# A new order of the steps on every engine, with new PSUM banks and six steps on other engines, in an attention and gated convolution kernel

## The chip, the cores and the metric

One core of a Trainium2 chip. The metric is the device time of one execution in microseconds (us), as the median of several runs; less is better. A measurement of this kernel tells a change of about 0.3% (0.7 us) from none.

## The reference: what is computed

Attention in which each query sees only the keys of its own cluster, followed by a feed-forward layer with a gated convolution along the sequence. Batch 4, 8 heads, 768 tokens, head size 64, 16 clusters; width 512, inner width 1024.

```python
q_assign = argmax(einsum('bhsd,hcd->bhsc', q_n, c_n))   # cluster of each query; k_assign likewise
mask = q_assign[:, :, :, None] == k_assign[:, :, None, :]
scores = where(mask, q @ k.T / sqrt(D), -1e9)
x = softmax(scores) @ v                                  # heads side by side: (4, 768, 512)
h = maximum(x @ w_in, 0)
conv_out = sum(conv_w[i] * h shifted by i - 1 along the sequence, i = 0, 1, 2)
out = (h * sigmoid(conv_out)) @ w_out
```

## The kernel before: tiles, stages and what sets the order

The attention works on 16 **groups** g (batch and pair of heads) and 32 **slots** t (a group and one half of its queries; a batch has 8 slots). The feed-forward layer follows batch by batch, while the attention of the next batches runs, so all engines hold both kinds of work for most of the span.

The order is written out in one long string, `PLAN`, of some 1650 tokens. `step` turns each token into the instructions of a function, and each engine executes its own in the order in which they stand there. No scheduler changes it; semaphores only make an engine wait. A token `T.3.0@2` carries indices and, behind the @, the PSUM bank (0 to 3, and 4 to 7 at the two ends), and a letter d, a or p says which engine copies: VectorE (DVE), ScalarE (ACT) or GpSimd (POOL). The tokens that the text speaks of, with the lines of the profile before:

- `_wz` (L665, L666) sets the operand of the dummy matmuls and a scratch column on DVE; `_k.n` (L663) issues n dummy matmuls on TensorE (PE), whose result nobody reads; `_zp`/`_zd` (L709) clear part of an `ext` buffer on POOL/DVE; `_id` makes the identity on POOL, `_par` (L668) reads it on DVE; `_n3` transposes the centroids.
- `LQ`, `LK`, `LV` load on SP's queue. `T.g.c` (L277) transposes four blocks of q and k of group g on PE, `Qa`/`Qd` (L233, L235) copy them to `qkT`; for the last six groups `D.g.o` (L285) transposes on DVE instead. `CDa`/`CDp`, `CQp` and `CVp` (L233, L235) cast q, k and v to half precision.
- `A.g` (L318): products of tokens and centroids on PE. `M0.g` to `M6.g` (L342 to L381): the argmax on DVE, ending in a `pack` of cluster numbers and their squares; groups 0 and 1 do it for each head apart (`M1.0.1`). `K.g` (L386) transposes the pack on PE, `Ba`/`Bd` copy it, `BX.g` sends it by DMA as three extra rows of `ext`, which make the mask part of the score product.
- `S.t.i` (L413): scores of slot t, in two double banks; `E.t.i` (L425): exponentials on ACT; `V.t.u` (L444): product with v; `NR.t` (L455) and `N.t` (L460): normalisation on DVE, which frees V's bank; `X`, `Y`, `XD`: the transposed x.
- `I` (L498) first feed-forward product, `R` (L511 on ACT, L513 on DVE) relu, `aw/bw/cw` and `a/b/c` (L530, L532) the three taps on DVE, `H` (L560) tanh on ACT, `G` (L569) gate on DVE, `O` (L581) second product, `F` and `FX` output.

For group 0 the first part reads: `T.0.0`, `T.0.1`, `T.0.2` with their copies, ten dummies, `A.0`, then the argmax of each head, while `T.1.*` runs on PE.

Of the kernel before, what the change touches and what calls it, by code (L numbers as in the profile page):

```python
# [177 lines left out]

# [686 lines left out]
```

## Time and profile before

| | us |
|---|---|
| median of 3 runs (lowest, highest) | 242.31 (241.92, 242.58) |
| the profiled execution | 240.97 |
| its span on the core | 239.2 |
| PE busy in the span | 228.5 |
| DVE busy | 209.8 |
| ACT busy | 209.5 |
| POOL busy | 71.0 |

The profile is of one execution. Its page gives the busy time of each engine; the chain of waits follows the work that ended last back from step to step; the timeline lists instructions with their start, length and the idle time ahead of them (in brackets, with what ended it); the table of stretches gives busy time between two times. Matmuls overlap, so that neighbours on PE are told by the distance of their starts.

### The profile page before, as it was taken

The numbers are of one execution on the slowest core, as the hardware profiler recorded it, in microseconds if no ns is written. First come the engines' busy times: TensorE is split into PE (matmuls) and PEld (weight loads), VectorE is DVE, ScalarE is ACT, GpSimd is POOL, SyncE is SP. The second block draws the span as 40 slices with busy tenths as digits, with TensorE's granted clock in tenths as the row PEclk, the third lists the DMA queues.
The fourth block names the chain that finished last, engine by engine and source line by source line (L and its number), as shares of the span: only waits on it lengthen the run. The fifth ranks groups of instructions, "written<-read, shape, count | busy, mean of one in ns | idle before, by whom it ended". The sixth has DMA issues, their size and how long they took to land.

```text
span 239.2 us, 6261 instructions
## 1 busy us (share of the span) xinstructions
PE 228.5 (96%) x2420; PEld 145.5 (61%) x2420; DVE 209.8 (88%) x417; ACT 209.5 (88%) x326; POOL 71.0 (30%) x120
## 2 busy tenths in 40 slices
PE   7889899999999999989999999999999999999993
PEld 6757567676766775645566556655656666665541
DVE  5689677766989999999999999999899999999950
ACT  3757899898999999989999999997999999987841
POOL 7348690974944004360200340007120000000000
PEclk9999999999999999999999999999999999999999
DMA  8966979899995957796578957885491104022233
GB/s 153 217 154 171 292 192 313 268 225 230 267 229 164 192 96 140 111 152 135 154 144 148 133 129 167 197 135 102 110 249 38 33 3 175 4 88 88 90 132 132
DMA packets 97481, 36.79 MB, mean 154 GB/s; under 512 B 88745, under 2 KB 91305, under 8 KB 97452
## 3 DMA queue, kind: packets, MB, share of 16 engines
q1 hardware_dynamic: 96524, 36.17, 66.4%
q8 instruction: 19, 0.31, 0.6%
q10 hardware_dynamic: 928, 0.23, 0.5%
q14 instruction: 10, 0.08, 0.1%
HBM read 23.11 MB, written 6.29 MB: 123 GB/s over the span
## 4 chain that ended last, share of the span: by engine, by line
PE 65%; DVE 24%; issue 4%; DMA 3%; SPq 1%; ACT 1%; DVEq 0%; ACTq 0%
PE sc L413 18%; PE flex L581 12%; PE flex L498 11%; PE flex L444 10%; DVE cnv L532 5%; PE flex L277 4%; DVE hg L569 3%; PE flex L318 3%; PE tail L581 3%; DMA qk_in<-in_k_dram 2%; PE tail L498 2%; DVE sim L342 2%; DVE val L357 2%; DVE qkT L285 2%; DVE hpad L513 1%
## 5 line engine op out<-in xcount | busy, mean ns | idle before, releaser
L425 ACT ACTIVATE attn<-sc 128x768 f16<-128x768 f32 x192 | 148.1, 829 | 8.7 <-PE sc L413 7.4
L413 PE MATMUL sc<-ext 128*128 128x384 f16 x384 | 90.4, 325 | 0.3
L532 DVE SCALAR_TENSOR_TENSOR cnv<-hpad,cwcol,cnv 128x768 f16<-128x768 f16 (+2 forms) x72 | 62.4, 890 | 0.1
L444 PEld LDWEIGHTS <-attn 128*128 128x128 f16 x1152 | 50.9, 97 | 17.3 <-issue 2.7
L444 PE MATMUL flex<-v,attn 128*128 128x65 f16 x1152 | 55.0, 193 | 0.4 <-DVE sim L342 0.4
L498 PE MATMUL flex<-xT,w_in 128*128 128x384 f16 x228 | 45.5, 325 | 0.3 <-DVE x L460 0.2
L235 POOL CAST c<-qkT 128x768 f16<-128x768 f32 x21 | 21.4, 1027 | 76.6 <-DVE qkT L285 22.9
L413 PEld LDWEIGHTS <-ext 128*128 128x128 f16 x384 | 31.3, 97 | 20.4 <-issue 7.9
L581 PE MATMUL flex<-w_out,hg 128*128 128x512 f16 x160 | 42.3, 379 | 0.0
L498 PEld LDWEIGHTS <-w_in 128*128 128x128 f16 x256 | 24.1, 97 | 16.2 <-issue 1.0
L569 DVE SCALAR_TENSOR_TENSOR hg<-th,hpad 128x768 f16<-128x768 f32 (+3 forms) x34 | 31.1, 919 | 0.4 <-ACT th L560 0.3
L581 PEld LDWEIGHTS <-hg 128*128 128x128 f16 x192 | 17.7, 98 | 16.2 <-issue 0.6
L560 ACT ACTIVATE th<-cnv 128x768 f32<-128x768 f16 (+2 forms) x30 | 25.9, 864 | 1.2 <-DVE cnv L532 1.0
L235 POOL CAST v<-v_in 128x768 f16<-128x768 f32 x16 | 15.9, 997 | 18.9 <-DMA v_in<-in_v_dram 14.1
L511 ACT ACTIVATE hpad<-flex 128x384 f16<-128x384 f32 x39 | 19.5, 536 | 0.4 <-PE flex L498 0.4
L277 PE MATMUL flex<-id,qk_in 128*128 128x128 f32 x120 | 17.5, 277 | 1.6 <-DMA qk_in<-in_k_dram 0.9
L460 DVE TENSOR_TENSOR x<-flex,rec 128x384 f16<-128x384 f32 x32 | 17.5, 547 | 0.2
L277 PEld LDWEIGHTS flex<-id,qk_in 128*128 128x128 f32 x120 | 13.4, 141 | 4.0 <-issue 1.1
L318 PE MATMUL flex<-qkT,cT 128*32 128x384 f32 x128 | 13.6, 498 | 1.6 <-DVE qkT L285 0.8
L235 DVE COPY qkT<-flex 128x512 f32<-128x512 f32 x15 | 10.1, 686 | 5.4 <-PE flex L277 5.3
L530 DVE TENSOR_SCALAR cnv<-hpad,cwcol 128x768 f16<-128x768 f16 (+2 forms) x36 | 14.5, 411 | 0.3 <-ACT th L560 0.2
L233 ACT ACTIVATE qkT<-flex 128x512 f32<-128x512 f32 x15 | 8.7, 603 | 5.3 <-PE flex L277 5.3
(81 smaller groups left out, 210.2 us busy)
## 6 DMA issues: line engine op xcount, KB each, us to landing
v_in<-in_v_dram SPq DMA_DIRECT2D x16, 384.0 KB, 4.6
ext<-c SPq DMA_DIRECT2D x24, 192.0 KB, 3.2
out_dram<-o_sb SPq DMA_DIRECT2D x9, 512.0 KB, 2.8
qk_in<-in_q_dram SPq DMA_DIRECT2D x20, 192.0 KB, 3.1
qk_in<-in_k_dram SPq DMA_DIRECT2D x9, 384.0 KB
qk_in<-in_k_dram SPq DMA_DIRECT2D x24, 96.0 KB, 2.3
qk_in<-in_q_dram SPq DMA_DIRECT2D x24, 96.0 KB, 3.8
w_sb<-in_moe_w_in_dram SPq DMA_DIRECT2D x4, 512.0 KB, 4.4
```

Of the source, the lines that this page charges most:

```text
L235: (nc.vector if name == "d" else nc.gpsimd).tensor_copy(out=to, in_=src)
L277: nc.tensor.transpose(bank[at][:, P * i : P * (i + 1)], qk_t[g][:, o, P * j : P * (j + 1)], id128[:])
L318: nc.tensor.matmul(bank[at][32 * j : 32 * (j + 1), 0:HS], lhsT=cT32[:, g % NPR, :], rhs=tokens[:, j], start=True, stop=True, skip_group_ch ...
L413: nc.tensor.matmul(s[:, n, 0:HS], lhsT=ext_b[g % NE][:, h, 1, P * (kt + n) : P * (kt + n + 1)], rhs=ext_b[g % NE][:, h, 0, HS * a : HS * ( ...
L425: nc.scalar.activation(attn[t, i // 3][:, kt : kt + 2, :], sc[(6 * t + i) % 2][:, :, 0:HS], AF.Exp, scale=0.125)
L444: nc.tensor.matmul(avp(at)[:, u, 0 : D + 1], lhsT=attn[t, h][:, kt, P * jq : P * (jq + 1)], rhs=v16_b[g % NE][:, h, kt, 0 : D + 1], start= ...
L498: nc.tensor.matmul(bank[at][:, 0:HS], lhsT=w_in16[:, r, 2 * u + f, :], rhs=xT[:, b % 2, r, HS * a : HS * (a + 1)], start=(r == 0), stop=(r ...
L511: nc.scalar.activation(to, src, AF.Relu)
L532: nc.vector.scalar_tensor_tensor(out=cnv, in0=src, scalar=w, in1=cnv, op0=ALU.mult, op1=ALU.add)
L560: nc.scalar.activation(th, cnv_t[key].rearrange("p (f s) -> p f s", s=N), AF.Tanh, scale=0.5)
L569: nc.vector.scalar_tensor_tensor(out=hg_b[b][:, 2 * u + fs.start : 2 * u + fs.stop, lo : lo + N], in0=th, scalar=1.0, in1=hpad(b, u)[:, fs ...
L581: nc.tensor.matmul(bank[at][:, 0:Dm], lhsT=hg_b[b][:, fb, P * tq : P * (tq + 1)], rhs=w_out16[:, fb, :], start=(fb == 0), stop=(fb == NFB ...
```

## The change

The string `PLAN` is replaced: 1654 tokens for 1656, in another order on each engine, 355 of them with another bank or name. Six steps go to another engine: the copies `Qa.0.0`, `Qd.0.1`, `Qd.5.0`, `Qd.6.2` become `Qd.0.0`, `Qa.0.1`, `Qa.5.0`, `Qa.6.2`; the relu `Ra.0.0` becomes `Rd.0.0`; the clearing `_zp.1.1` becomes `_zd.1.1`. `_wz` stays on DVE but goes behind `_par`. The dummy matmuls go from 113 to 87: the first burst from 35 to 14, the others by five in all.

Besides, the number 24 is taken out of the argmax's sixth step and put into the table that the fourth multiplies with, so that the sixth has one arithmetic operation for two; and `transposes`, `load` and `argmax` get branches for the groups in `RUNS` and `PSUM_PAIRS`, which are both empty, so that no group takes them.

```diff
+PSUM_PAIRS = ()
+RUNS = ()
...
-    "_wz _zp.0.1 LQ.0.0 _zd.1.0 _hpk.0 _zp.1.1 _id _zd.4.0 _par LQ.0.1 LK.0.1 _pk.2 _hz.3 _v.0 _zp.0.0 _v.2 "
-    "_hz.1 _cent lk.0.0 _n0 _n1 _nq _n2 _k.35@4 T.0.0@1 Qa.0.0 T.0.1@0 _id16 Qd.0.1 T.0.2@2 _n3@1 _n4 Qa.0.2 "
+    "_hz.1 _pk.2 _zp.0.1 LQ.0.0 _zd.1.0 _hpk.0 _zd.1.1 _id _zd.4.0 _par _wz LQ.0.1 LK.0.1 _v.0 _v.2 _zp.0.0 "
+    "_cent lk.0.0 _n0 _n1 _nq _n2 _k.14@4 T.0.0@0 Qd.0.0 T.0.1@1 _id16 Qa.0.1 T.0.2@2 Qa.0.2 _n3@3 _n4 _k.10@4 "
...
+    MIDDLE = -8.5 * SHARP
...
             nc.vector.tensor_scalar(
                 out=pack[:, first : first + G].rearrange("p (h u) -> p h u", h=n),
-                in0=best,
-                scalar1=-8.5,
-                scalar2=SHARP,
+                in0=mx_t[key].rearrange("p u h -> p h u"),
+                scalar1=MIDDLE,
+                scalar2=None,
                 op0=ALU.add,
-                op1=ALU.mult,
...
-                out=iota16[:], in0=iota32[:], scalar1=-1.0, scalar2=16.0, op0=ALU.mult, op1=ALU.add
+                out=iota16[:], in0=iota32[:], scalar1=-SHARP, scalar2=16.0 * SHARP, op0=ALU.mult, op1=ALU.add
```

At three places the order reads as follows.

DVE at the very start, before (warm is the dummies' operand, ext the buffers that are cleared, par and sq, nrm the preparation of the centroids):

```order
L665 MEMSET warm 128x64
L666 MEMSET scratch 128x1
L709 MEMSET ext_96 64x768
L709 MEMSET ext_99 64x768
L668 TENSOR_REDUCE par_c<-id_78 128x2
L674 TENSOR_TENSOR sq_c<-cent 128x64
L675 TENSOR_REDUCE nrm_c<-sq_c 128x1
```

The same place after:

```order
L758 MEMSET ext_96 64x768 x2
L758 MEMSET ext_99 64x768
L717 TENSOR_REDUCE par_c<-id_78 128x2
L714 MEMSET warm 128x64
L715 MEMSET scratch 128x1
L723 TENSOR_TENSOR sq_c<-cent 128x64
```

Three clearings and `par` now stand ahead of the dummies' operand, where it stood first.

ACT ahead of the first exponentials, before (spk is the copy of the pack of group 0, qkT the copies of group 2, ext the cast `CDa.1.0.1` and at the end `CDa.1.0.0`, attn the exponentials of slot 0):

```order
L233 ACTIVATE spk<-flex_69 36x128
L233 ACTIVATE qkT<-flex_69 128x512
L233 ACTIVATE ext_96<-qkT 64x768
L233 ACTIVATE qkT<-flex_67 128x512
L233 ACTIVATE qkT<-flex_68 128x512
L425 ACTIVATE attn<-sc_73 128x768
L425 ACTIVATE attn<-sc_77 128x768
L233 ACTIVATE ext_96<-qkT 64x768
```

The same place after:

```order
L236 ACTIVATE spk<-flex_66 36x128
L236 ACTIVATE ext_96<-qkT 64x768
L236 ACTIVATE qkT<-flex_66 128x512
L236 ACTIVATE qkT<-flex_69 128x512
L236 ACTIVATE qkT<-flex_68 128x512
L474 ACTIVATE attn<-sc_73 128x768
L236 ACTIVATE ext_96<-qkT 64x768
L474 ACTIVATE attn<-sc_77 128x768
```

One cast moves ahead of the first copy of group 2, and the other ahead of the second exponential.

DVE ahead of the argmax of group 10, before (hg is a gate, cnv a tap, qkT the two transposes `D.10.0` and `D.10.1`, rec and x16 the normalisation of slot 13):

```order
L569 SCALAR_TENSOR_TENSOR hg_1638<-th_1764,hpad1_111 128x768
L532 SCALAR_TENSOR_TENSOR cnv_1784<-hpad2_112,cwcol_86,cnv_1784 128x768
L455 RECIPROCAL rec_1878<-flex3_69 128x6
L285 STREAM_TRANSPOSE qkT_1880<-qk_in_1743 128x768
L532 SCALAR_TENSOR_TENSOR cnv_1784<-hpad2_112,cwcol_86,cnv_1784 128x768
L460 TENSOR_TENSOR x16_1883<-flex3_69,rec_1878 128x2x3x64
L285 STREAM_TRANSPOSE qkT_1880<-qk_in_1743 128x768
```

The same place after:

```order
L581 SCALAR_TENSOR_TENSOR cnv_1759<-hpad2_112,cwcol_86,cnv_1759 128x768
L504 RECIPROCAL rec_1851<-flex1_67 128x6
L306 STREAM_TRANSPOSE qkT_1853<-qk_in_1717 128x768
L618 SCALAR_TENSOR_TENSOR hg_1607<-th_1741,hpad1_111 128x768
L581 SCALAR_TENSOR_TENSOR cnv_1759<-hpad2_112,cwcol_86,cnv_1759 128x768
L306 STREAM_TRANSPOSE qkT_1853<-qk_in_1717 128x768
L509 TENSOR_TENSOR x16_1858<-flex1_67,rec_1851 128x2x3x64
```

The gate goes behind the first transpose, and the second transpose ahead of the normalisation; what stands ahead of the argmax of group 10 in all stays the same.

More of the change, by code (lines that the diff above doesn't have):

```diff
@@ L251, in load @@
             )
+        elif g in RUNS:
+            tv = to[:, o, :].rearrange("p (h x) -> p h x", h=2)
+            if part is None:
+                queue.dma_start(tv, src[b, h0 : h0 + 2].rearrange("h (p j) d -> p h (j d)", p=P))
+            elif o:
+                queue.dma_start(tv[:, part], src[b, h0 + part].rearrange("(p j) d -> p (j d)", p=P))
+            else:
+                tv = tv[:, part].rearrange("p (j y) -> p j y", y=2 * D)
+                queue.dma_start(tv, src[b, h0 + part].rearrange("(j p t) d -> p j (t d)", p=P, t=2))
         elif part is None:
@@ L276, in transposes @@
             o, j = divmod(4 * c + i, J)
+            if g in RUNS:
+                to = bank[at][:, P * i : P * (i + 1)]
+                if o == 0:
+                    to = bank[at][:, P * (i - i % 2) : P * (i - i % 2 + 2)]
+                    to = to.rearrange("p (x t) -> p t x", t=2)[:, i % 2]
+                first = HS + D * j - D
+                nc.tensor.transpose(to, qk_t[g][:, o, first : first + P], id128[:])
+                nc.tensor.transpose(to[0:D], qk_t[g][:, o, D * j : D * (j + 1)], id128[:])
+                continue
             nc.tensor.transpose(
@@ L338, in sim, with room_of, small @@
             return x if h is None else x[:, :, h : h + 1]
+        room = bank[sims_at[g]] if g in PSUM_PAIRS else None
+        def room_of(first):
+            x = room[:, first : first + 24].rearrange("p (u h) -> p u h", h=2)
+            return x if h is None else x[:, :, h : h + 1]
+        def small(x):
+            return x[:, 0:G].rearrange("p (u h) -> p u h", h=n)
         if i == 0:
@@ L343, in argmax @@
         elif i == 1:
-            mx_t[key] = rot.tile([P, 24], F32, name="mx", tag="mx", bufs=BUFS["mx"])
-            nc.vector.tensor_reduce(
-                out=mx_t[key][:, 0:G].rearrange("p (u h) -> p u h", h=n), in_=sim(), axis=AX.X, op=ALU.max
-            )
-        elif i == 2:
-            eq_t[key] = rot.tile([P, 24 * C], F16, name="eqq", tag="eqq", bufs=BUFS["eqq"])
-            mx = mx_t.pop(key)[:, 0:G].rearrange("p (u h) -> p u h", h=n).unsqueeze(3).to_broadcast((P, 12, n, C))
-            nc.vector.tensor_tensor(out=shape(eq_t[key]), in0=sim(), in1=mx, op=ALU.is_equal)
+            if room is None:
+                mx_t[key] = small(rot.tile([P, 24], F32, name="mx", tag="mx", bufs=BUFS["mx"]))
+            else:
+                mx_t[key] = room_of(HS)
@@ new lines, in argmax @@
+            nc.vector.tensor_reduce(out=mx_t[key], in_=sim(), axis=AX.X, op=ALU.max)
+        elif i == 2:
+            if room is None:
+                eq_t[key] = shape(rot.tile([P, 24 * C], F16, name="eqq", tag="eqq", bufs=BUFS["eqq"]))
+            else:
+                x = room[:, 0 : 24 * C].rearrange("p (u h c) -> p u h c", h=2, c=C)
+                eq_t[key] = x if h is None else x[:, :, h : h + 1]
+            mx = mx_t.pop(key).unsqueeze(3).to_broadcast((P, 12, n, C))
+            nc.vector.tensor_tensor(out=eq_t[key], in0=sim(), in1=mx, op=ALU.is_equal)
@@ L352, in argmax @@
         elif i == 3:
             val_t[key] = rot.tile([P, 24 * C], F16, name="val", tag="val", bufs=BUFS["val"])
-            iota = iota16[:].unsqueeze(1).to_broadcast((P, G, C))
-            eq = eq_t.pop(key)[:, 0 : G * C].rearrange("p (u c) -> p u c", c=C)
-            val = val_t[key][:, 0 : G * C].rearrange("p (u c) -> p u c", c=C)
-            nc.vector.tensor_tensor(out=val, in0=eq, in1=iota, op=ALU.mult)
-        elif i == 4:
-            mx_t[key] = rot.tile([P, 24], F32, name="best", tag="best", bufs=BUFS["best"])
-            val = val_t.pop(key)[:, 0 : G * C].rearrange("p (u c) -> p u c", c=C)
-            nc.vector.tensor_reduce(out=mx_t[key][:, 0:G], in_=val, axis=AX.X, op=ALU.max)
+            if n == 1:
+                iota = iota16[:].unsqueeze(1).to_broadcast((P, 12, C))
+                nc.vector.tensor_tensor(
+                    out=shape(val_t[key])[:, :, 0], in0=eq_t.pop(key)[:, :, 0], in1=iota, op=ALU.mult
+                )
+            else:
+                iota = iota16[:].unsqueeze(1).to_broadcast((P, 24, C))
+                eq = eq_t.pop(key).rearrange("p u h c -> p (u h) c")
+                val = val_t[key][:].rearrange("p (u c) -> p u c", c=C)
+                nc.vector.tensor_tensor(out=val, in0=eq, in1=iota, op=ALU.mult)
+        elif i == 4:
+            if room is None:
+                mx_t[key] = small(rot.tile([P, 24], F32, name="best", tag="best", bufs=BUFS["best"]))
+            else:
+                mx_t[key] = room_of(HS + 24)
+            nc.vector.tensor_reduce(out=mx_t[key], in_=shape(val_t.pop(key)), axis=AX.X, op=ALU.max)
@@ L362, in argmax @@
         elif i == 5:
-            best = mx_t.pop(key)[:, 0:G].rearrange("p (u h) -> p h u", h=n)
             first = 24 if h is None else 64 * h + 12
@@ L366, in argmax @@
                 out=pack[:, first : first + G].rearrange("p (h u) -> p h u", h=n),
-                in0=best,
-                scalar1=-8.5,
-                scalar2=SHARP,
+                in0=mx_t[key].rearrange("p u h -> p h u"),
+                scalar1=MIDDLE,
+                scalar2=None,
                 op0=ALU.add,
-                op1=ALU.mult,
             )
-        elif h is None:
-            u = pack[:, 24:48].rearrange("p (h o c) -> p o h c", h=2, o=2)
-            to = pack[:, 0:108].rearrange("p (x y) -> p x y", y=54)[:, :, 0:24]
-            to = to.rearrange("p x (h o c) -> p x h o c", h=2, o=2)[:, :, :, 0, :]
-            nc.vector.tensor_tensor(out=to, in0=u, in1=u, op=ALU.mult)
-        else:
-            u = pack[:, 64 * h + 12 : 64 * h + 24].rearrange("p (o c) -> p o c", o=2)
-            to = pack[:, 64 * h : 64 * h + 60].rearrange("p (x y) -> p x y", y=30)[:, :, 0:J]
-            nc.vector.tensor_tensor(out=to, in0=u, in1=u, op=ALU.mult)
+        else:
+            best = mx_t.pop(key).rearrange("p (o c) h -> p o h c", o=2)
+            if h is None:
+                u = pack[:, 24:48].rearrange("p (h o c) -> p o h c", h=2, o=2)
+                to = pack[:, 0:108].rearrange("p (x y) -> p x y", y=54)[:, :, 0:24]
+                to = to.rearrange("p x (h o c) -> p x h o c", h=2, o=2)[:, :, :, 0, :]
+            else:
+                best = best[:, :, 0]
+                u = pack[:, 64 * h + 12 : 64 * h + 24].rearrange("p (o c) -> p o c", o=2)
+                to = pack[:, 64 * h : 64 * h + 60].rearrange("p (x y) -> p x y", y=30)[:, :, 0:J]
+            if room is None:
+                nc.vector.tensor_tensor(out=to, in0=u, in1=u, op=ALU.mult)
+            else:
+                for x in [slice(None)] if n == 1 else range(2):
+                    nc.vector.scalar_tensor_tensor(
+                        out=to[:, x], in0=best[:, x], scalar=MIDDLE, in1=u[:, x], op0=ALU.add, op1=ALU.mult
+                    )
     def turn(g, h, at):
```

230 rows, old and new, of the table PLAN are left out of this document.

## The prediction

> **What bounds the kernel now.** I read the page's busy times first, then the table of stretches.
>
> ```profile
> PE 228.5 (96%) x2420; PEld 145.5 (61%) x2420; DVE 209.8 (88%) x417; ACT 209.5 (88%) x326; POOL 71.0 (30%) x120
> ```
>
> ```profile
> 0.00:36.00 36.00, 30.63 (x351) 22.74 (x355) 26.54 (x70) 25.36 (x38) 23.66 (x59) 1.00 0.86 197
> 36.00:84.00 48.00, 47.99 (x580) 32.91 (x573) 39.78 (x90) 44.64 (x67) 24.78 (x41) 1.00 0.92 236
> 84.00:108.00 24.00, 22.76 (x279) 15.15 (x278) 24.00 (x42) 23.34 (x39) 8.90 (x7) 1.00 0.84 124
> 108.00:228.00 120.00, 119.63 (x1188) 71.52 (x1185) 117.08 (x214) 113.12 (x180) 13.67 (x14) 1.00 0.52 116
> ```
>
> The columns are the stretch, its length, then the busy time of PE, PE's weight loads, DVE, ACT and POOL. PE idles 5.37 us in the first 36, 0.01 in the next 48, 1.24 where DVE is busy for 24.00 of 24.00 us, and 0.37 in the 120 up to 228. So from 36 us on two engines are full in turns, and no order of the same work brings more than some 1.6 us there. The opening is where an order can win or lose; any delay in it goes to the end nearly whole, because PE has nothing behind it to catch up with.
>
> The chain of waits in the opening (start, length, what):
>
> ```profile
> 1.83 4.87 DMA qk_in<-in_k_dram
> 6.83 0.84 PE flex L277 x6
> 7.79 0.56 PE sc L663 x10
> 8.37 0.90 PE flex L318 x8
> 9.36 0.59 DVE sim L342
> 19.39 0.23 PE flex L386
> 31.60 0.23 PE flex L386
> ```
>
> It is the first k, its transposes on PE with ten dummies (L663) and `A.0` (L318) behind them, then DVE's argmax of one group after another (it begins with sim at 9.36), up to the packs that PE turns, `K.1.0` at 19.39 and `K.3` at 31.60.
>
> **The change, part by part.** The sum is made against the profiled execution, 240.97 us with a span of 239.2; the median of the runs is 1.34 longer, and I put the sum on the median, 242.31.
>
> *The first copies.* ACT now copies the second and third chunk of group 0; before, DVE took the second beside it.
>
> ```profile
> 7.28 0.69 DVE L235 COPY qkT<-flex 128x512 f32<-128x512 f32 x1 [1.96 <-PE flex L277]
> 7.72 0.60 ACT L233 ACTIVATE qkT<-flex 128x512 f32<-128x512 f32 x1 [1.37 <-PE flex L277]
> ```
>
> On ACT the second runs from 7.28 to 7.88, and the third to 8.48 for 8.32. `A.0` waits for it, and all of DVE's chain for `A.0`: +0.16 us, with bounds of 0 (if the chain has that slack somewhere) and 0.6 (a whole copy).
>
> *The cast ahead of group 2's copies on ACT.*
>
> ```profile
> 14.94 0.60 ACT L233 ACTIVATE qkT<-flex 128x512 f32<-128x512 f32 x1 [2.10 <-PE flex L277]
> 15.56 0.84 ACT L233 ACTIVATE ext<-qkT 64x768 f16<-64x768 f32 x1
> 19.98 0.81 ACT L425 ACTIVATE attn<-sc 128x768 f16<-128x768 f32 x1 [0.49 <-PE sc L413]
> ```
>
> The cast of 0.84 goes into the idle 2.10, so the copies behind it, and the first exponential, start up to 0.8 earlier. But the third exponential, at 19.98, waits for `S.0.2`, which stands behind `K.1.0` in PE's order both times, and that one for DVE's argmax (19.39 in the chain). What ACT gains it waits away there: 0, at best the idle 0.49.
>
> *DVE's argmax.* The steps of groups 0 to 3 keep their number; halves are interleaved otherwise. The sixth loses an arithmetic operation but is still one pass over the same 12 or 24 elements (its rows stand with the first rival): 0. `NR.0` moves into the wait for `K.3`:
>
> ```profile
> 31.86 0.22 DVE L235 COPY spk<-flex 72x128 f16<-72x128 f16 x1 [0.32 <-DMA qk_in<-in_k_dram]
> 32.76 0.18 DVE L455 RECIPROCAL rec<-flex 128x6 f32<-128x6 f32 x1
> ```
>
> The reciprocal of 0.18 goes from ahead of the next copy to `qkT`, which PE's transposes wait for, into the idle 0.32: −0.18, or 0 where PE comes late anyway; I take −0.18.
>
> *The dummies and their operand.* Five later dummies go, 0.06 each (the chain's ten in 0.56), out of places where PE mostly waits: −0.1, between −0.3 and 0. The first burst is cut to 14 and starts late:
>
> ```profile
> 0.81 0.11 DVE L665 MEMSET warm<- 128x64 uint32 x1 [0.81 <-PEq L849]
> 0.98 3.40 PE L663 MATMUL sc<-warm 128*128 128x128 f16 x35 [0.98 <-DVE scratch L666]
> 1.16 1.50 DVE L709 MEMSET ext<- 64x768 f32 x2 [0.23 <-issue]
> 3.18 0.29 DVE L668 TENSOR_REDUCE par_c<-id 128x2 f32<-128x128 f32 x1 [0.51 <-POOL id masks.py:199]
> 5.08 0.85 PE L277 MATMUL flex<-id,qk_in 128*128 128x128 f32 x6 [0.71 <-POOL iota L699]
> ```
>
> Three clearings of 0.75 from 0.81 on end at 3.06, `par` at 3.35, the operand and scratch at about 3.5: the burst starts there instead of at 0.98. As work it costs 0, since at their slowest pace (below) 14 end at 5.0, and the first transposes start at 5.08. Queued behind `par` and `_wz` on DVE stand the steps on the centroids, some 0.2 late, whose result PE takes behind the transposes of 6.83 only: 0.
>
> *The stall at 104 us.* DVE's `D.10.1` goes ahead of `N.13`:
>
> ```profile
> 103.54 0.54 DVE L460 TENSOR_TENSOR x<-flex,rec 128x384 f16<-128x384 f32 x1
> 104.01 0.96 DVE L285 STREAM_TRANSPOSE qkT<-qk_in 128x768 f32<-128x768 f32 x1
> 105.02 0.85 PE L318 MATMUL flex<-qkT,cT 128*32 128x384 f32 x8 [0.79 <-DVE qkT L285]
> 106.69 0.57 DVE L342 STREAM_TRANSPOSE sim<-flex 128x384 f32<-128x384 f32 x1
> 107.31 0.35 PE L444 MATMUL flex<-v,attn 128*128 128x65 f16 x6 [0.35 <-DVE sim L342]
> ```
>
> `A.10` on PE can start 0.47 earlier. But `V.15.0` at 107.31 uses the bank of `A.10` before and after, waits for `M0.10` to read it, and ahead of `M0.10` stands the same DVE work in both orders. PE then waits 0.47 longer at 107.31: 0, at best −0.5. The same holds wherever DVE is full: its steps ahead of the argmax of each group from 7 on are the same in both orders, but for the copies of groups 5 and 6 and the relu that change engines, and those lie in the stretch from 36 to 84, where DVE idles 8.22 us and ACT 3.36. So they bring 0 on DVE and cost 0 on ACT, with PE full; without that cover two copies of 0.60 on ACT would cost 1.2.
>
> The sum: +0.16 + 0 − 0.18 − 0.1 + 0 = −0.12, so **242.2 us**, no change within 0.3% (about what a measurement of this kernel can tell, 0.7 us).
>
> **The rivals.** *First, faster: fewer collisions between DVE and POOL.* Some DVE steps take far longer when a POOL cast runs:
>
> ```profile
> 11.79 0.17 DVE L365 TENSOR_SCALAR hpack<-best 128x12 f16<-128x12 f32 x1
> 12.09 0.16 DVE L381 TENSOR_TENSOR hpack<-hpack 128x12 f16<-128x12 f16 x1
> 12.32 0.82 POOL L235 CAST ext<-qkT 64x768 f16<-64x768 f32 x1 [1.99 <-ACT qkT L233]
> 12.66 0.60 DVE L365 TENSOR_SCALAR hpack<-best 128x12 f16<-128x12 f32 x1
> 13.14 0.82 POOL L235 CAST ext<-qkT 64x768 f16<-64x768 f32 x1
> 13.30 0.68 DVE L381 TENSOR_TENSOR hpack<-hpack 128x12 f16<-128x12 f16 x1
> 16.03 0.26 DVE L357 TENSOR_TENSOR val<-eqq,iota 128x192 f16<-128x192 f16 x1
> 17.54 0.89 DVE L357 TENSOR_TENSOR val<-eqq,iota 128x192 f16<-128x192 f16 x1
> ```
>
> The stretched ones end where the casts end (13.26 for 13.14, 13.98 for 13.96). These three pay 0.43, 0.52 and 0.63 us on the chain, 1.58 in all, and others stand between them and 32 us. The new order puts POOL's `CVp.1` behind two casts of group 2 and shifts ACT's copies that release them, so the collisions fall differently. If two of the three go, the gain is about 1.1 us: 241.1. For it: each one removed counts in full. Against it: POOL casts as much as before in the same stretch, and both engines start from the same copies. The Trainium skill, "SBUF — State Buffer", section "Who interferes with whom", says the same as a rule: GpSimd and DVE steps with two SBUF inputs, or in a two-port mode, lock each other out for a whole instruction, whoever comes second waits. By that rule L365, L381 and L357 collide with a cast, and the rows agree (0.60 for 0.17, 0.68 for 0.16, 0.89 for 0.26); which of them meets a cast in a new order, it doesn't tell.
>
> *Second, slower: PE's clock is not up when the first k arrives.* The table's clock column stands at 1.00 throughout, yet dummies run at two paces:
>
> ```profile
> 2.77 0.95 PE L663 MATMUL sc<-warm 128*128 128x128 f16 x7
> 3.82 0.55 PE L663 MATMUL sc<-warm 128*128 128x128 f16 x7
> L663 PE MATMUL sc<-warm x80: 219/219/314, 1.0 to 14.7; 128*128 128x128 f16 x80
> ```
>
> Seven take 0.95 us from 2.77, one alone up to 0.31, so they start 0.107 apart; from 3.82 on it is (0.55 − 0.22) / 6 = 0.055. The pace doubles between 3.4 and 3.8, that is 2.4 to 2.8 us after the first dummy. In the new order the first dummy comes at 3.5, so the double pace would come at 5.9 to 6.3 if the transposes count as work like the dummies: before 6.83, at no price. If they don't, it comes later. Then from 6.83 on everything takes twice its time: the transposes some 0.7 more (0.84 in the chain), ten dummies 1.07 for 0.56, so `A.0` starts near 9.4 for 8.37 and takes some 0.8 more (0.90 in the chain): DVE's chain is up to 1.8 us late, and with it the end. It decides from a change of pace at about 8.3 us, where half the excess passes 0.7. I price it at 1.2, two thirds of the whole: 243.4. For it: 14 dummies for 35, and the operand behind three clearings. Against it: PE is nearly without a gap from 3.5 on. The Trainium skill, "TensorE: Matmul & The Clock Gate", speaks for this rival: by "Part 1: The HAM clock gate (the "warmup" mystery)" the array runs at half rate until a free-running window of about 3.4 us was busy, so that the moment differs from run to run, and by "Part 4: PE-mode transpose" transposes don't count as busy in it. By the first rule the trace agrees roughly (2.4 to 2.8 us, for a window of 3.4); the second is shown by no row. By both together an estimate is that the full rate comes near 10 us, and the sum is about 244; by the trace's own 2.8 us it is 242.2.
>
> **How the numbers follow.** The forecast, 242.2, has 0.40: the two full engines hold what they have. Its own range is 241.5 to 242.9. Fewer collisions, 241.1, has 0.34, and reaches to 240.4 if more than these three go. The slow clock, 243.4, has 0.26, and reaches to 244.0. The range that leaves out 2 in 10 goes from 240.6 to 243.6. Faster by over 0.3% has the 0.34, slower the 0.26, no change the 0.40.
>
> **What would show it.** Right: PE idles over 4 us in the first 36 and under 2 after; the first `M0` starts at 9.5 us; the stall ahead of `A.10` shrinks to 0.3 and the one at `V.15.0` grows by as much; `K.3` comes within 0.5 us of 31.60. For the first rival, L365, L357 and L381 would show shorter stretched rows before 32 us, and `K.3` would come near 30.5. For the second, the ten dummies ahead of `A.0` would take about 1.1 us and `A.0` would start past 9. The prediction is wrong in its ground if a gain or loss over 0.7 us arises behind 36 us, with PE's idle time there changed by as much.

## The result and the profile after

The changed kernel takes 244.95 us (median of 22 runs, 242.48 to 248.48), the kernel before in the same rounds 241.87 (22 runs, 240.00 to 244.41). The ratio is 1.0119, with a 95% interval of 1.0098 to 1.0140: 1.2% slower, about 2.9 us. Executions over 1.5% longer than the fastest of the same kernel count as slow ones and are left out of the ratios. I had forecast 242.2 and no change, with a range up to 243.6. The forecast was wrong, and its range too short on the slow side.

The profiled executions took 240.97 before and 243.56 after (spans 239.2 and 241.8). The second is 1.39 us under the median of its kernel, the first 0.9 under its own. The changed kernel's times are also more spread. So one trace of it shows one case out of several, and this turned out to matter.

The busy times and the stretches of the profile after, with the columns as before:

```profile
PE 226.9 (94%) x2394; PEld 143.9 (60%) x2394; DVE 210.0 (87%) x417; ACT 210.1 (87%) x327; POOL 69.5 (29%) x119
```

```profile
0.00:36.00 36.00, 28.80 (x321) 20.82 (x321) 27.41 (x71) 24.82 (x38) 23.50 (x59) 1.00 0.86 195
36.00:84.00 48.00, 46.87 (x552) 31.94 (x552) 37.40 (x88) 44.35 (x66) 23.98 (x40) 1.00 0.94 237
84.00:108.00 24.00, 22.94 (x292) 15.51 (x291) 24.00 (x40) 23.16 (x39) 7.56 (x7) 1.00 0.72 117
108.00:228.00 120.00, 118.37 (x1187) 71.25 (x1186) 116.50 (x214) 113.18 (x179) 14.48 (x15) 1.00 0.54 114
```

DVE and ACT are as busy as before, within 0.3%, and POOL has 1.5 us less to do. PE's idle time goes from 0.01 to 1.13 us between 36 and 84, and from 0.37 to 1.63 behind 108. The prediction had called just this, a loss over 0.7 us behind 36 us with PE's idle time changed by as much, the sign that its ground is wrong. But the 1.12 us between 36 and 84 are one wait for a transfer, shown next, which turned out to be chance; the sign came up partly by luck.

The rows of PE on which its steps can be followed, from the timeline after:

```profile
3.68 1.67 PE L712 MATMUL sc<-warm 128*128 128x128 f16 x14 [3.68 <-DVE scratch L715]
5.22 2.43 PE L298 MATMUL flex<-id,qk_in 128*128 128x128 f32 x12
7.60 0.72 PE L712 MATMUL sc<-warm 128*128 128x128 f16 x10
8.39 0.85 PE L339 MATMUL flex<-qkT,cT 128*32 128x384 f32 x8
31.68 0.23 PE L435 MATMUL flex<-id,pack 128*128 128x128 f16 x1 [0.61 <-DVE pack L425]
74.65 0.63 PE L298 MATMUL flex<-id,qk_in 128*128 128x128 f32 x4 [1.14 <-DMA qk_in<-in_q_dram]
106.33 0.85 PE L339 MATMUL flex<-qkT,cT 128*32 128x384 f32 x8 [0.68 <-DVE qkT L306]
109.42 0.73 PE L493 MATMUL flex<-v,attn 128*128 128x65 f16 x18 [0.93 <-DVE sim L372]
```

In this execution the opening is nearly untouched: `A.0` at 8.39 (8.37 before), `K.3` at 31.68 (31.60). The wait of 1.14 us for q of group 8, absent before, takes the kernel to +1.32 at `A.8` (77.03 for 75.71). The stall ahead of `A.10` falls from 0.79 to 0.68, but the wait at `V.15.0` grows from 0.35 to 0.93, and `M0.10` is 2.11 late, where `A.10` was 1.31 late. What is left of the 2.6 comes in small pieces behind that.

### The profile page after: what moved, and what is told of

The parts are those of the page before. It is cut to its first block, busy times and chain, and to the rows that moved or that the text cites. A ratio compares the mean times of both kernels' runs of the same rounds, so it can differ in the third digit from the quotient of the medians.

```text
span 241.8 us, 6220 instructions
## 1 busy us (share of the span) xinstructions
PE 226.9 (94%) x2394; PEld 143.9 (60%) x2394; DVE 210.0 (87%) x417; ACT 210.1 (87%) x327; POOL 69.5 (29%) x119
## 4 chain that ended last, share of the span: by engine, by line
PE 66%; DVE 21%; DMA 5%; issue 4%; ACT 2%; SPq 1%; ACTq 0%; DVEq 0%
PE sc L462 17%; PE flex L630 13%; PE flex L493 11%; PE flex L547 10%; PE flex L298 4%; DVE cnv L581 4%; PE flex L339 3%; PE tail L630 3%; DMA qk_in<-in_q_dram 3%; DVE hg L618 2%; DMA out_dram<-o_sb 2%; PE tail L547 2%; DVE sim L372 1%; DVE hpad L562 1%; DVE eqq L386 1%
## 5 line engine op out<-in xcount | busy, mean ns | idle before, releaser
L581 DVE SCALAR_TENSOR_TENSOR cnv<-hpad,cwcol,cnv 128x768 f16<-128x768 f16 (+2 forms) x72 | 63.3, 904 | 0.1
L238 POOL CAST c<-qkT 128x768 f16<-128x768 f32 x21 | 19.2, 922 | 78.6 <-DVE qkT L306 44.8
L618 DVE SCALAR_TENSOR_TENSOR hg<-th,hpad 128x768 f16<-128x768 f32 (+3 forms) x34 | 31.7, 939 | 0.6 <-ACT th L609 0.5
L560 ACT ACTIVATE hpad<-flex 128x384 f16<-128x384 f32 x39 | 20.1, 537 | 0.8 <-PE flex L547 0.7
L298 PE MATMUL flex<-id,qk_in 128*128 128x128 f32 x120 | 18.0, 284 | 1.2 <-DMA qk_in<-in_q_dram 1.1
L509 DVE TENSOR_TENSOR x<-flex,rec 128x384 f16<-128x384 f32 x32 | 17.4, 547 | 0.2
L236 ACT ACTIVATE qkT<-flex 128x512 f32<-128x512 f32 x17 | 9.8, 600 | 5.7 <-PE flex L298 4.2
L372 DVE STREAM_TRANSPOSE sim<-flex 128x384 f32<-128x384 f32 x16 | 9.2, 577 | 4.8 <-PE flex L339 4.1
```

Source lines behind the costliest of these rows:

```text
L238: (nc.vector if name == "d" else nc.gpsimd).tensor_copy(out=to, in_=src)
L298: nc.tensor.transpose(bank[at][:, P * i : P * (i + 1)], qk_t[g][:, o, P * j : P * (j + 1)], id128[:])
L560: nc.scalar.activation(to, src, AF.Relu)
L581: nc.vector.scalar_tensor_tensor(out=cnv, in0=src, scalar=w, in1=cnv, op0=ALU.mult, op1=ALU.add)
L618: nc.vector.scalar_tensor_tensor(out=hg_b[b][:, 2 * u + fs.start : 2 * u + fs.stop, lo : lo + N], in0=th, scalar=1.0, in1=hpad(b, u)[:, fs ...
```

## The experiments

Of the first two theories, one took the trace at its word: the wait for q comes from `K.6`, which now stands later, behind `T.7.0`, so that the issue of `BX.6` on SP, and the loads of group 8 behind it, come 0.7 us later (`BX.6` at 65.01 for 64.30). The other took the prediction's slower rival, PE's clock, for the cause. Each kernel is either the changed one with a piece put back, or the kernel before with a piece of the change; "the kernel with the new opening" is a case of the second. Ratios are to the kernel before, which ran beside each, with their 95% intervals.

**K.6 put back** in the changed kernel:

```diff
-T.7.1@0 S.8.3 Qd.7.1 T.7.2@1
+T.7.1@0 K.6@3 S.8.3 Qd.7.1 Bd.6 T.7.2@1
...
-T.7.0@2 K.6@0 Bd.6 E.8.2
+T.7.0@2 E.8.2
```

> The changed kernel with one piece of its order undone: the sums and casts of K.6 (K.6 on PE, Bd.6 on VectorE) stand behind T.7.1 again, as in the kernel before, and with them the issue of BX.6 on SP. Queue theory (K.6 moved early puts BX.6 later... or its wait in front of the loads of k and q of group 8 on SP, and PE then waits for q at 74 us): the wait of 1.14 us ahead of group 8's transposes of q goes, and the time falls by about 1.0 us against the changed kernel, to about 244.0 us. Opening theory (the loss is PE's clock, which comes up later in most executions behind the short and late first burst): no change, within 0.3 us of the changed kernel.

1.0119 (1.0074 to 1.0165, six runs): nothing comes back that can be told, though the interval just leaves room for the 1.0 us of the theory.

**K.6 moved** in the kernel before, the same edit the other way round:

```diff
-T.7.1@3 K.6@1 Qd.7.1 Bd.6 S.8.3
+T.7.1@3 Qd.7.1 S.8.3
...
-T.7.0@2 E.8.2
+T.7.0@2 K.6@3 Bd.6 E.8.2
```

> The kernel before with only K.6 and Bd.6 moved to stand behind T.7.0, so that BX.6 and the loads of group 8 behind it on SP come about 0.7 us later. Queue theory: about 1.0 us slower than the kernel before, 242.9 us, with a wait of about 1 us for q ahead of group 8's transposes. Opening theory: the same as the kernel before, within 0.3 us.

1.0015 (0.9988 to 1.0041). SP's queue and PE in that kernel:

```profile
65.40 0.79 SPq L396 DMA_DIRECT2D ext<-spk  x1
66.23 0.69 SPq L253 DMA_DIRECT2D qk_in<-in_k_dram  x1
66.96 2.03 SPq L257 DMA_DIRECT2D qk_in<-in_q_dram  x2
```

```profile
73.74 0.63 PE L277 MATMUL flex<-id,qk_in 128*128 128x128 f32 x4
```

`BX.6` comes at 65.40 for 64.30 before, as the theory says (some 0.4 of it is that this whole execution runs late: `A.7` at 67.00 for 66.58), yet PE doesn't wait for q at all: the move is real and the wait isn't its rule. The 1.0 us of the theory would be a ratio of 1.0041, the very end of the interval. The next kernel leaves `K.6` in its new place in the changed order, and there too the transposes come without a wait:

```profile
73.16 0.64 PE L298 MATMUL flex<-id,qk_in 128*128 128x128 f32 x4
```

The most visible loss of the trace was the chance of one execution, and the first theory falls as an account of the 2.9 us.

**The operand put first again** in the changed kernel:

```diff
-_hz.1 _pk.2 _zp.0.1 LQ.0.0 _zd.1.0
+_wz _hz.1 _pk.2 _zp.0.1 LQ.0.0 _zd.1.0
...
-_par _wz LQ.0.1
+_par LQ.0.1
...
-_k.14@4
+_k.35@4
```

> The changed kernel with the opening's operand put back: the clearing of _wz stands first on VectorE and the first burst counts 35 dummy products instead of 14, as in the kernel before. Opening theory: 1 to 2 us back against the changed kernel, about 243.5 us, and less spread from run to run. Queue theory: no change, within 0.3 us, since the wait at 74 us and the slow steps at 105 us stay.

1.0092 (1.0054 to 1.0131). Perhaps a part comes back, most doesn't.

**The operand late** in the kernel before:

```diff
-_wz _zp.0.1 LQ.0.0 _zd.1.0 _hpk.0 _zp.1.1 _id _zd.4.0 _par
+_zp.0.1 LQ.0.0 _zd.1.0 _hpk.0 _zd.1.1 _id _zd.4.0 _par _wz
...
-_k.35@4
+_k.14@4
```

> The kernel before with only the opening changed: the clearing of _wz stands behind _par and the clearings ahead of it, and the first burst counts 14 dummy products. Opening theory: 0.5 to 1.8 us slower than the kernel before, about 243 us. Queue theory: the same as the kernel before, within 0.3 us, 241.9 us.

1.0015 (0.9991 to 1.0040): by itself it costs nothing that can be told. So neither theory holds alone. I next cut the order into four stretches, and gave the kernel before the new order in one at a time (banks renamed at the seams).

**The opening alone**, up to `M3.4`; of its diff three places that the text speaks of:

```diff
-M1.1.1 M2.1.1 M3.1.1 M1.1.0 M4.1.1
+M1.1.1 M1.1.0 M2.1.1 M3.1.1 M4.1.1
...
-M3.1.0 M6.1.1 _k.2@0 A.2@2 K.1.1@1 M4.1.0 M5.1.0 M6.1.0
+M3.1.0 M4.1.0 M5.1.0 M6.1.1 A.2@2 S.0.1 _k.9@1 K.1.1@3 M6.1.0
...
-_zp.2.1 CVp.1 CDp.2.0.1
+_zp.2.1 CDp.2.0.0 CDp.2.0.1 CVp.1
```

> The kernel before with the changed order up to M3.4 (about 37 us), then its own. Place theory (the loss of 2.9 us is a sum over places: opening with late clock, the loads of group 8, the VectorE steps at 105 us): 0.3 us of it is here in every execution and 1.2 us more in those in which PE's clock comes up late, so 0.5 to 1.5 us slower than the kernel before. Rival (no place costs much by itself, the loss needs the whole new order together, or comes from the argmax's other arithmetic, which this kernel doesn't have): within 0.3 us of the kernel before.

1.0068 (1.0042 to 1.0094), 1.6 us. More than half of the loss is here, and the trace of this kernel shows it, where the trace of the changed kernel had not. PE's rows:

```profile
8.70 0.85 PE L317 MATMUL flex<-qkT,cT 128*32 128x384 f32 x8
19.66 0.23 PE L385 MATMUL flex<-id,hpack 128*128 128x128 f16 x1 [0.99 <-DVE hpack L380]
26.05 0.85 PE L317 MATMUL flex<-qkT,cT 128*32 128x384 f32 x8 [1.40 <-DVE pack L376]
```

The last of them in the kernel before, and group 2's product with the iota on DVE there:

```profile
24.46 0.85 PE L318 MATMUL flex<-qkT,cT 128*32 128x384 f32 x8 [0.42 <-DVE qkT L235]
21.41 0.36 DVE L357 TENSOR_TENSOR val<-eqq,iota 128x384 f16<-128x384 f16 x1
```

`A.0` is 0.33 late, `A.3` 1.59, and it waits 1.40 us for DVE. (The row at 19.66 is `K.1.1`.) DVE and POOL in the kernel with the new opening:

```profile
16.96 0.82 POOL L234 CAST ext<-qkT 64x768 f16<-64x768 f32 x1 [1.30 <-ACT qkT L232]
17.05 0.94 DVE L350 TENSOR_TENSOR eqq<-sim,mx 128x192 f16<-128x192 f32 x1
20.99 1.92 POOL L234 CAST ext<-qkT 64x768 f16<-64x768 f32 x2
22.26 1.63 DVE L356 TENSOR_TENSOR val<-eqq,iota 128x384 f16<-128x384 f16 x1
22.86 0.82 POOL L234 CAST v<-v_in 128x768 f16<-128x768 f32 x1
```

Group 2's product with the iota takes 1.63 us for 0.36. It starts while the second of the two casts of `ext` runs (21.75 to 22.90), sits that one out, and then the cast of v too, which follows without a gap; it ends at 23.89, just behind that cast (23.68).

**From M3.4 to M1.8 alone** (37 to 78 us):

```diff
...
-T.5.0@1 Qd.5.0
+T.5.0@1 Qa.5.0
...
```

> The kernel before with the changed order from M3.4 to M1.8 alone (about 37 to 78 us). Place theory: 0.3 to 1.0 us slower, as the wait of about 1 us for q of group 8 falls into some executions. Rival: within 0.3 us.

0.9986 (0.9962 to 1.0010). The 0.3 to 1.0 us expected here would be above this interval.

**From M1.8 to N.15 alone** (78 to 113 us):

```diff
...
-NR.13 D.10.0 bw.0.2.1 N.13 D.10.1 bw.0.3.1
+NR.13 D.10.0 Gw.0.1.1 bw.0.2.1 D.10.1 N.13 bw.0.3.1
...
```

> The kernel before with the changed order from M1.8 to N.15 alone (about 78 to 113 us). Place theory: 0.6 to 0.8 us slower in every execution, with PE waiting about 0.9 us ahead of V.15.0 for the similarity's argmax on VectorE, where it waits 0.35 us before. Rival: within 0.3 us.

1.0010 (0.9983 to 1.0038). PE does wait longer at `V.15.0`, 1.42 us, but `A.10` comes 0.68 early in this kernel, so that `M0.10` is only 0.39 late. The 0.6 to 0.8 us expected here are neither seen nor excluded.

**From N.15 to the end alone** (113 us on):

```diff
...
-CQp.11.1 M4.10 M5.10 E.16.5
+CQp.11.1 M4.10 V.16.0 V.16.1 M0.11 M5.10
...
```

> The kernel before with the changed order from N.15 to the end alone (about 113 us on). Place theory: 0 to 0.4 us slower, from the tail. Rival (the loss lies behind 113 us in executions other than the profiled one): 1 us or more slower.

0.9968 (0.9945 to 0.9991), which seemed a gain (but see below).

**The opening put back** in the changed kernel, everything up to `M3.4`:

```diff
-_hz.1 _pk.2 _zp.0.1 LQ.0.0
+_wz _zp.0.1 LQ.0.0
...
```

> The changed kernel with the order of the kernel before up to M3.4 (about 37 us): the complement of h1_opening. Opening theory (the new order of the opening makes the loss, behind it the new order is worth nothing): within 0.5 us of the kernel before, perhaps faster by what the three later stretches gave when each was moved alone (sum -0.8 us). Rival (the loss needs the opening and the rest together, or the argmax's other arithmetic costs): half of the loss or more stays, 1.3 us or more slower than the kernel before.

1.0027 (0.9997 to 1.0057), against 1.0119 with the new opening. The opening is the larger part from this side too. Which piece of it?

**The casts alone** in the kernel before:

```diff
-_pk.2 _hz.3 _v.0
+_pk.2 _v.0
...
-_zp.2.0 _zp.3.1 _zp.3.0 _zp.2.1 CVp.1 CDp.2.0.1
+_zp.2.0 _hz.3 _zp.3.1 _zp.3.0 _zp.2.1 CDp.2.0.0 CDp.2.0.1 CVp.1
...
-_cw1@2 CDp.2.0.0 BX.2
+_cw1@2 BX.2
```

> The kernel before with only four GpSimd steps moved as in the change: the casts of group 2 (CDp.2.0.0, CDp.2.0.1) ahead of v's cast CVp.1, which waits for its transfer, and _hz.3 behind a clearing. Collision theory (the casts now run while VectorE does group 2's argmax, whose product with the iota was 0.36 us and becomes 0.86 to 1.63): 0.5 to 1.2 us slower than the kernel before. Rival (the opening loses by the late first burst, or by the order of the argmax's steps): within 0.3 us.

0.9991 (0.9963 to 1.0019). Alone it costs nothing that can be told. In its trace the product starts at 21.38, 0.04 us ahead of the two casts, and takes 0.36.

**The casts put back** in the kernel with the new opening, the product's 1.63 us being the reason:

```diff
...
-_zp.2.1 CDp.2.0.0 CDp.2.0.1 CVp.1
+_zp.2.1 CVp.1 CDp.2.0.1 CDp.2.0.0
...
```

> h1_opening (the kernel before with the changed order up to M3.4) with these GpSimd steps put back: v's cast CVp.1 ahead of the casts of group 2, _hz.3 at the start. Collision theory: 0.5 to 1.2 us faster than h1_opening, 242.3 to 243.0 us, the product of group 2 with the iota at 0.36 us again. Rival: as h1_opening, within 0.3 us of 243.5.

1.0044 (1.0013 to 1.0075). In its profiled execution the product takes 0.36 again (from 21.82), and `A.3` is on time, at 24.47, although the operand is late and `A.0` starts at 8.63. But this execution, 241.41 us, is the second fastest of the kernel's twelve (median 242.33).

**The operand put first** in the kernel with the new opening:

```diff
...
-_par _wz LQ.0.1
+_par LQ.0.1
...
-_k.14@4
+_k.35@4
```

> h1_opening with the clearing of _wz first on VectorE and 35 dummy products again. Clock theory (the late and short first burst costs): 0.3 to 0.6 us faster than h1_opening in all executions and more in those with a late clock, 242.9 us or less, and A.0 at 8.4 us. Collision theory: half a step only by luck of the phase, since the casts and the argmax still run at one time: within 0.5 us of 243.5.

1.0028 (1.0000 to 1.0055). Its profiled execution has `A.0` at 8.37, as before, and yet `A.3` is 1.52 late:

```profile
8.37 0.85 PE L317 MATMUL flex<-qkT,cT 128*32 128x384 f32 x8
25.98 0.85 PE L317 MATMUL flex<-qkT,cT 128*32 128x384 f32 x8 [1.40 <-DVE qkT L234]
```

The product takes 1.63 us here too. So the collisions cost it without any late clock. The ratios of this and the last kernel lie between, with intervals that touch that of the whole opening.

**Both put back** in the kernel with the new opening, the two edits above together:

```diff
...
-_zp.2.1 CDp.2.0.0 CDp.2.0.1 CVp.1
+_zp.2.1 CVp.1 CDp.2.0.1 CDp.2.0.0
...
-_par _wz LQ.0.1
+_par LQ.0.1
...
```

> h1_opening (the changed order up to M3.4, then the old one) with both pieces put back. Theory of the two together: the same as the kernel before, within 0.3%, 241.1 to 241.9 us, with group 2's product with the iota at 0.36 us and A.3 at 24.5 us. Rival (the argmax's order): 0.4% or more slower than the kernel before.

1.0013 (0.9996 to 1.0029), wholly below the interval of the new opening, and this is the firmest result on the opening. DVE, POOL and PE in this kernel, at the place where the product took 1.63:

```profile
21.45 0.36 DVE L356 TENSOR_TENSOR val<-eqq,iota 128x384 f16<-128x384 f16 x1
```

```profile
21.91 0.82 POOL L234 CAST v<-v_in 128x768 f16<-128x768 f32 x1 [1.05 <-DMA v_in<-in_v_dram]
22.68 1.59 POOL L234 CAST ext<-qkT 64x768 f16<-64x768 f32 x2
```

```profile
24.11 0.85 PE L317 MATMUL flex<-qkT,cT 128*32 128x384 f32 x8 [0.19 <-ACT qkT L232]
```

POOL idles 1.05 us for v's transfer, and in that gap DVE's product runs free, 0.36 us. The old order of POOL, with a waiting cast in front, had kept POOL out of DVE's way; `A.3` is at 24.11.

**Both in the kernel before**, with nothing else:

```diff
...
-_zp.2.0 _zp.3.1 _zp.3.0 _zp.2.1 CVp.1 CDp.2.0.1
+_zp.2.0 _hz.3 _zp.3.1 _zp.3.0 _zp.2.1 CDp.2.0.0 CDp.2.0.1 CVp.1
...
-_zd.4.0 _par LQ.0.1
+_zd.4.0 _par _wz LQ.0.1
...
```

> The kernel before with the two opening pieces of the change together and nothing else: _wz late with 14 dummy products, and the casts of group 2 ahead of CVp.1. Pair theory (the two together make the opening's loss): 0.4 to 0.7% slower than the kernel before. Rival (it takes the new order of the argmax's steps on VectorE as well): within 0.3%.

1.0010 (0.9985 to 1.0035). **The argmax's order alone** in the kernel before:

```diff
...
-M1.1.1 M2.1.1 M3.1.1 M1.1.0 M4.1.1
+M1.1.1 M1.1.0 M2.1.1 M3.1.1 M4.1.1
...
-M3.1.0 M6.1.1 _k.2@0
+M3.1.0 M4.1.0 M5.1.0 M6.1.1 _k.2@0
...
```

> The kernel before with only the order of the argmax's steps of groups 0 to 2 on VectorE as in the change (M1.1.0 ahead of M2.1.1, M4.1.0 and M5.1.0 ahead of M6.1.1, M0.2 ahead of Bd.1.1). Argmax theory: 0.4 to 1.0% slower, since K.1.1 stands behind two more steps and the steps fall under GpSimd's casts. Theory of the two pieces: within 0.3% of the kernel before.

1.0019 (0.9992 to 1.0046). No piece costs anything that can be told alone, and the pair neither; the loss of the opening takes the pieces together. The traces suggest why: with the casts alone and with the pair the product starts 0.04 and 0.09 us ahead of the casts and takes 0.36; in the whole new opening the casts start 1.27 us ahead of the product (20.99 and 22.26).

**Both put back in the changed kernel:**

```diff
...
-_zp.2.1 CDp.2.0.0 CDp.2.0.1 CVp.1
+_zp.2.1 CVp.1 CDp.2.0.1 CDp.2.0.0
...
-_k.14@4
+_k.35@4
```

> The changed kernel with both pieces of the opening put back: _wz first and 35 dummy products, and v's cast CVp.1 ahead of the casts of group 2 on GpSimd. Theory of the two together (late start and casts push the argmax of groups 1 and 2 under GpSimd's casts): 1.5 to 2.5 us of the loss goes, at most 0.4% over the kernel before, 242.0 us or less. Rival (the argmax's order on VectorE makes the loss): over 0.7% over the kernel before, as with _wz put back alone.

1.0068 (1.0043 to 1.0094, six runs): against 1.0119, 1.2 us come back, less than the theory said.

**The stretch from 78 to 113 us put back as well:**

```diff
...
-NR.13 D.10.0 Gw.0.1.1 bw.0.2.1 D.10.1 N.13 bw.0.3.1
+NR.13 D.10.0 bw.0.2.1 N.13 D.10.1 bw.0.3.1
...
```

> The changed kernel with three things put back: _wz first with 35 dummy products, CVp.1 ahead of the casts of group 2, and the whole order from M1.8 to N.15 (about 78 to 113 us). Sum theory (two opening pieces and the stretch at 105 us make the loss): within 0.3% of the kernel before, 241.4 to 242.1 us if the kernel before is at 241.4, and PE waits 0.35 us at V.15.0 as in the kernel before. Rival (the rest of the loss is spread over the whole new order or comes from the argmax's other arithmetic): 0.5% or more over the kernel before.

1.0002 (0.9974 to 1.0031): the loss is gone, within 0.3%, with the new order of everything else, the banks and the argmax's other arithmetic still in place.

What happens at 105 us, in the changed kernel, DVE first and then POOL:

```profile
102.97 0.91 DVE L618 SCALAR_TENSOR_TENSOR hg<-th,hpad 128x768 f16<-128x768 f32 x1
103.81 1.57 DVE L581 SCALAR_TENSOR_TENSOR cnv<-hpad,cwcol,cnv 128x768 f16<-128x768 f16 x1
105.31 0.97 DVE L306 STREAM_TRANSPOSE qkT<-qk_in 128x768 f32<-128x768 f32 x1
106.20 0.52 DVE L509 TENSOR_TENSOR x<-flex,rec 128x384 f16<-128x384 f32 x1
106.64 1.33 DVE L581 SCALAR_TENSOR_TENSOR cnv<-hpad,cwcol,cnv 128x768 f16<-128x768 f16 x1
```

```profile
103.17 1.41 POOL L238 CAST c<-qkT 128x768 f16<-128x768 f32 x1 [1.89 <-DVE qkT L306]
106.34 0.82 POOL L238 CAST c<-qkT 128x768 f16<-128x768 f32 x1 [0.48 <-DVE qkT L306]
```

And with the stretch put back, DVE, POOL and PE (this execution, 243.11 us, is the second longest of twelve and late from the start, with `A.0` at 9.93, so its rows are compared with each other and not with the times above):

```profile
104.36 0.97 DVE L581 SCALAR_TENSOR_TENSOR cnv<-hpad,cwcol,cnv 128x768 f16<-128x768 f16 x1
105.25 0.54 DVE L509 TENSOR_TENSOR x<-flex,rec 128x384 f16<-128x384 f32 x1
105.72 0.96 DVE L306 STREAM_TRANSPOSE qkT<-qk_in 128x768 f32<-128x768 f32 x1
106.61 0.97 DVE L581 SCALAR_TENSOR_TENSOR cnv<-hpad,cwcol,cnv 128x768 f16<-128x768 f16 x1
```

```profile
104.55 1.47 POOL L238 CAST c<-qkT 128x768 f16<-128x768 f32 x1 [1.89 <-DVE qkT L306]
106.75 1.52 POOL L238 CAST c<-qkT 128x768 f16<-128x768 f32 x1
```

```profile
109.02 0.35 PE L493 MATMUL flex<-v,attn 128*128 128x65 f16 x6 [0.35 <-DVE sim L372]
```

The same taps and casts in the kernel before:

```profile
102.65 0.97 DVE L532 SCALAR_TENSOR_TENSOR cnv<-hpad,cwcol,cnv 128x768 f16<-128x768 f16 x1
104.90 0.97 DVE L532 SCALAR_TENSOR_TENSOR cnv<-hpad,cwcol,cnv 128x768 f16<-128x768 f16 x1
```

```profile
103.15 1.15 POOL L235 CAST c<-qkT 128x768 f16<-128x768 f32 x1 [2.20 <-DMA ext<-c]
105.03 1.52 POOL L235 CAST c<-qkT 128x768 f16<-128x768 f32 x1 [0.15 <-DVE qkT L285]
```

The two taps (L581, L532 before) meet two casts each time. Before, they start 0.50 and 0.13 us ahead of their casts and take 0.97. With the stretch put back each tap starts 0.1 to 0.2 us ahead, takes 0.97 again, and the cast pays (1.47, 1.52 for 0.82 alone). In the new order each cast starts first and the tap pays, 1.57 and 1.33: 0.60 + 0.36 = 0.96 us more on DVE, which is full there, and PE waits 0.93 for 0.35 at `V.15.0`. The transposes `D.10.0` and `D.10.1` release the casts (the first cast before waits for a transfer besides). In the new order `Gw.0.1.1` (0.91, L618) stands between the first of them and its tap, and `N.13` (0.52, L509) between the second and its own: so much lead the casts get.

The wait at `V.15.0` goes with the stretch in every trace of this document: 0.35 us in all fourteen kernels with its old order, 0.93 or 1.42 in all six with the new one. From the start of `A.9` to that of `M0.10` the fourteen take 15.15 to 15.30 us, the six 15.76 to 16.08. The two with 15.76 and 15.78 are those with the old opening and the new stretch; there only the second tap is stretched (1.59 us), the first takes 1.00.

**The later stretches together** in the kernel before, since one of them had seemed faster:

```diff
...
-T.5.0@1 Qd.5.0
+T.5.0@1 Qa.5.0
...
```

> The kernel before with the changed order in the two stretches that were not slower alone: M3.4 to M1.8 and N.15 to the end. If their effects add (0.14% and 0.32% faster, each with an interval of about 0.25%): 0.3 to 0.5% faster than the kernel before, about 240.4 us. Rival (both were chance): within 0.2%.

1.0006 (0.9976 to 1.0035). The gain of the last stretch is not seen again, and no version beats the kernel before.

## Why the prediction was wrong

**What bounds the kernel** held: DVE and ACT full in turns, PE behind them, and a delay of the opening going to the end (in the trace of the new opening alone `A.3` is 1.59 us late and `A.15` 2.36). The conclusion drawn from it didn't: "no order of the same work brings more than some 1.6 us" speaks of gains only. Full engines limit what an order can win, not what it can lose.

**The step that failed** is the one on the same DVE work: at the stall of 104 us "ahead of `M0.10` stands the same DVE work in both orders", so 0, and for the argmax "still one pass over the same 12 or 24 elements: 0". The steps were the same, their durations were not. At 105 us the same tap took 1.33 to 1.57 us for 0.97, and `M0.10` lost 0.80 beyond what `A.10` had lost. With that stretch put back beside the two opening pieces, the ratio goes from 1.0068 to 1.0002; that the stretch costs time there is shown. The ratios tell its worth by itself less well: 0.7% by these two, at most 0.6% by the kernel with the old opening, and 0.1% (up to 0.4%) in the kernel before. In the last two traces `A.10` had gained 0.6 us on the way from `A.9`, which took back a part of it. The distance from `A.9` to `M0.10`, 0.5 to 0.9 us longer in all six traces, puts it at 0.2 to 0.4%, an estimate that agrees with these ratios.

**The first rival had the mechanism and the wrong sign.** It priced the stretched rows of the trace before, each of which could only vanish, and gave a gain the chance of 0.34. The order can as well bring new ones: at group 2's product it made 1.63 us of 0.36 in the kernel with the new opening, and 0.86 in the profiled execution of the changed kernel:

```profile
21.46 0.86 DVE L398 TENSOR_TENSOR val<-eqq,iota 128x384 f16<-128x384 f16 x1
```

It also named the very move, `CVp.1` behind two casts of group 2, but weighed it for a gain only, and "POOL casts as much as before" against that. It is the wait in front of the casts that counted, not their number. That the casts' move plays a part is shown with the operand's (both put back: 1.0068 to 1.0013); that the move makes it alone is refuted (0.9991).

**The second rival, PE's clock,** cost nothing in the profiled execution: ten dummies in 0.72 us, `A.0` at 8.39. In the kernel with `K.6` put back, whose opening is that of the changed kernel, the trace shows it as predicted:

```profile
3.69 1.68 PE L712 MATMUL sc<-warm 128*128 128x128 f16 x14 [3.69 <-DVE scratch L715]
5.42 2.80 PE L298 MATMUL flex<-id,qk_in 128*128 128x128 f32 x12
8.23 1.27 PE L712 MATMUL sc<-warm 128*128 128x128 f16 x10
9.43 1.01 PE L339 MATMUL flex<-qkT,cT 128*32 128x384 f32 x8
```

The dummies take 1.27 us, `A.0` starts past 9 and `M0.0` is 1.23 late. This trace holds a loss of the whole size: `K.3` is 1.78 late (33.38), 1.06 of it by `A.0`, the stretch at 105 us adds 0.80 (`A.10` 1.64 late, `M0.10` 2.44), and the span is 2.6 us longer. But the late operand isn't needed for it. With the stretch put back the operand stands first, and the ten dummies are as slow:

```profile
8.73 1.27 PE L712 MATMUL sc<-warm 128*128 128x128 f16 x10
```

Over all traces `A.0` starts at 8.25 to 8.43 in thirteen kernels with the operand first and at 9.93 in this one; with the operand late it starts at 8.39, 8.63, 8.67, 8.70, 8.96 and 9.43. From these I estimate 0.3 to 0.5 us for the late operand. So the rival is mostly an event of some executions; as a lasting price on the old order it is under 0.4% (late operand in the kernel before: 1.0015, up to 1.0040). In the new opening the early operand brought the ratio from 1.0068 to 1.0028, with touching intervals. How the pieces need each other, say by a late start that pushes group 1's argmax under the casts (a cast at 16.96, DVE's comparison of 0.94 us at 17.05), is argued, not shown.

**The other terms** were too small to tell. `K.3` came at 31.68 (within 0.5 of 31.60, as said, though by the luck of this execution: 33.38 with `K.6` put back), `M0.0` at 9.38 for 9.5, and the stall ahead of `A.10` shrank by 0.11, not by 0.47. **Left out altogether** was SP's queue behind `K.6`. The trace after made that look like the chief mistake, with a wait of 1.14 us; by itself it cost nothing that two runs could tell, and their intervals end at about the 1.0 us that it was thought to cost.

**What stays open:** how the opening's loss splits over its pieces, since it needs them together; what an execution of the changed kernel near its median loses in the opening, since the profiled ones with its opening have `K.3` at 31.68, 31.70 (operand put first) and 33.38; and whether the argmax's other arithmetic, which was never changed alone, is worth anything within the 0.3% that the run with all three put back leaves.

## What to carry to other kernels

When an order is changed, what engines do at the same time must be priced as well as what stands behind what: a step that costs 0.97 us in one neighbourhood costs 1.57 in another, and a wait at the head of one engine's queue can be what keeps it out of another's way. Where times of one kernel differ by 3 us from run to run, the largest wait of a single trace is a suspect and no more; moving it by itself, in both directions, cost two runs. Where no piece is slow alone, cut the change into stretches, put them in and take them out, and look for the smallest set whose removal brings the old time back.
